# Lightning attention and four summed experts on one core: values of a chunk and scores of the next in one TensorE run

## Chip, core and metric

The kernel runs on one core of one Trainium2 chip. The metric is the device time of one execution in microseconds (us). Three timed executions before the change took 1149.92, 1150.4 and 1151.87 us, so the median is 1150.4 us. One further execution was recorded by the hardware profiler; times of single instructions come from that one.

## What is computed

All numbers are fp32. The first block is a linear attention with decay over 4 batches, 8 heads, 768 positions and 64 columns per head, in blocks of 64 positions that pass a 64x64 state per head on:

```python
for b in range(nb):                      # 12 blocks of 64 positions
    intra = einsum('bhic,bhjc->bhij', qb, kb) * Dmask
    intra = einsum('bhij,bhjd->bhid', intra, vb)
    inter = einsum('bhid,bhde->bhie', qb * lam_pow, kv_state)
    out[:, :, sl] = intra + inter
    kv_state = lam_block * kv_state + einsum('bhsd,bhse->bhde', kb * rev_pow, vb)
```

Its output, turned to 3072 tokens of 512 columns, goes through four experts that are all applied and summed with normalised weights:

```python
p = domain_probs / (domain_probs.sum(-1, keepdims=True) + 1e-09)
for e in range(4):
    h = maximum(x @ w1[e], 0.0)          # 512 -> 1024
    out += p[:, e:e + 1] * (h @ w2[e])   # 1024 -> 512
```

## The kernel before

**Tokens and units.** The 24 chunks of 128 tokens (two blocks of 64 each, all eight heads) form three groups of 8 chunks. A unit is one group with one expert, so there are twelve, numbered 0 to 11 in the order in which they run. Both matrix products of a unit are built with Strassen's scheme in Winograd's form: seven products M1 to M7 of operands that are blocks (A11, A12, A22, B11 and so on) or sums of blocks (S1 to S4 and T1 to T4). The first product (`x @ w1`) carries the scheme two levels deep. The second product (`h @ w2`) has one level in units 0 to 4 and two levels ("nested") from unit 5 on.

**Steps and slots.** TensorE's order is written out by hand in the main loop. While unit `at` does its second product, the next unit does its first. Each unit has seven steps `i`, one for a product of each kind, and each step has eight slots `x`. In units 0 to 4 the even slots 0, 2, 4 and 6 each hold a quarter of the second product (`part`, matmuls of line 1175) and the odd slots hold two of the first product's inner products (`inner`, line 1116; slot 5 holds only one). So a unit has 56 slots, and slot number `(at * 7 + i) * 8 + x` counts through all units. Behind a slot's matmuls the loop issues at most a few waiting pieces of VectorE work, then the attention steps that stand at this slot, then due transfers (`pump`).

**Waiting VectorE work.** `lately` holds the attention's pieces, `background` the operands of later products and sums, `own_sums` operand sums of the first product. In units 0 to 3 one piece of `lately` is issued in each slot if there is one; then one of `background` if nothing was taken, if `fits()` (a planner's account of VectorE time, `filled`, is less than 0.6 slots ahead) or if more than one is queued; then `own_sums` under the like rule. What a product needs and has not been issued is forced at the product (`rest(force=True)`).

**Second product's order.** `SEQ2` is M1, M7, M4, M6, M2, M5, M3. M1, M6, M5 and M3 add up in PSUM banks `q01` and `q11`; M7, M4 add up in `q02` and `q12`, and M2 uses these two banks afresh. `part` (line 1175) evicts every quarter with a VectorE instruction of 128x256 (lines 1189 and 1193). `later_operands` (L899 on) queues S2 at step M4, S1 at step M2 and S4 at step M5, four VectorE instructions of 128x512 each; S4 takes S2 out of use. For unit 4 S4 goes through PSUM banks `q02` and `q12` (`through`).

**Attention of the groups 1 and 2** (chunks 8 to 23) is spread over units 0 to 3, one chunk every 12 slots from slot 24 (`BEGIN`). With s the chunk's slot:

- s - 10: `load_more` issues the loads of q and k on the SP queue (for group 2 transposed copies `qx` and `kx` and a plain k); s - 6: the load of v.
- s: `turn`. For group 1 TensorE transposes q and k into banks `s0` and `s1` (line 691), ScalarE copies both out (lines 699, 700), VectorE makes `qs`, the decayed q, from PSUM, and GpSimd decays k (`decayed`). For group 2 VectorE transposes `qx` and `kx` (line 673) and makes `qs`; k's decay is issued at s - 2. GpSimd carries a chunk's state on (`begin_state`).
- s + 5 (s + 6 in group 2): `scores`, 64 records of 64x64 matmuls into `s0` and `s1` (lines 721 and 728): q against k, and k against v for the state. Its VectorE pieces are masking (two instructions), `middle` (adds to the state) and `end` (state times decay, then an addition: two instructions of 128x256).
- s + 10 (s + 12 in group 2): `values`, 64 records of 64x64 matmuls into `s0` and `s1` (lines 775 and 793). ScalarE copies the output (line 814), VectorE adds what lies apart (`adds`). After every second chunk GpSimd and SP make and store operand sums (`pair_sums`), which `x_fill` reads back later.

A trace record is half of an fp32 matmul instruction, so four matmuls show as x8. All tiles of 128x512 named `small` share one pool of 42 buffers; a state is one such tile with two halves.

Of the kernel before, what the change touches and what calls it, by code (L numbers as in the profile page):

```python
# [21 lines left out]
def kernel(  # L22
# [456 lines left out]
    def comes_across(n):  # L479
        return where(n)[0] >= SECOND  # L480
# [150 lines left out]
    def fits():  # L631
        return filled[0] - now[0] < 0.6

    def rest(n=1, force=False):
        for _ in range(n):
            take(background, force)
# [18 lines left out]

    def begin_state(n):
        if where(n)[0] == 0 and n not in states:
            states[n] = small("kv")[:].rearrange("p (x h d) -> p x h d", x=2, d=D)
        if where(n)[0] and n in states and n not in carried:
            carried.add(n)  # L660
            passed(nc.gpsimd, states[n][:, 1], states[n][:, 0])

    def turn_across(n):

        qT, kT = nat.pop((n, "qx")), nat.pop((n, "kx"))
        qs = small("qs")

        def scaled():
            scale_q(qs, qT)
            turned[n] = qT, kT, qs  # L670

        def across(x):
            nc.vector.transpose(out=x[:], in_=x[:])
            vector(W, False)

        soon(n, *(lambda x=x: across(x) for x in (qT, kT)), scaled)

    def turn(n, tags):
        all_added()
        begin_state(n)  # L680
        if comes_across(n):
            turn_across(n)
            return
        if n < CPG:
            decayed(n)
        qn, kn = nat.pop((n, "q")), nat[n, "k"]
        qp = bank(tags[0], "qp")
        kp = bank(tags[1], "kp")
        for x, y in ((qp, qn), (kp, kn)):
            for ac in range(NHP):  # L690
                nc.tensor.transpose(  # L691
                    out=x[:, ac * C:(ac + 1) * C], in_=y[:, 2 * ac:2 * ac + 2].rearrange("p r d -> p (r d)"),
                    identity=ident[:],
                )
        if n >= CPG:
            decayed(n)
        del nat[n, "k"]
        qT, kT, qs = small("qT"), small("kT"), small("qs")
        nc.scalar.copy(out=qT[:], in_=qp[:])
        nc.scalar.copy(out=kT[:], in_=kp[:])  # L700
        scaled = lambda: scale_q(qs, qp)
        soon(n, scaled)
        turned[n] = qT, kT, qs, scaled

    def scores(n, tags):
        all_added()
        while n not in turned:
            take(lately, True)
        qT, kT = turned[n][0:2]
        while any(f in lately for f in turned[n][3:]):  # L710
            take(lately, True)
        begin_state(n)
        kd, vn = nat.pop((n, "kd")), nat[n, "v"]
        first, last = where(n)[0] == 0, where(n)[0] == NCH - 1

        sp = [bank(tags[r], "sp") for r in range(2)]
        blk = [slice(x * BL, (x + 1) * BL) for x in range(2)]
        for ac in range(NHP):
            for r in range(2):
                for x in range(2):  # L720
                    nc.tensor.matmul(  # L721
                        out=sp[r][half[x], ac * BL:(ac + 1) * BL], lhsT=hc(kT)[half[r], ac, blk[x]],
                        rhs=hc(qT)[half[r], ac, blk[x]], start=(ac == 0), stop=True, skip_group_check=True,
                    )
        for ac in range(NHP):
            for x in range(1 if last else 2):
                for r in range(2):
                    nc.tensor.matmul(  # L728
                        out=sp[x][half[r], 256 + ac * D:256 + (ac + 1) * D], lhsT=kd[half[x], 2 * ac + r],
                        rhs=vn[half[x], 4 * r + ac], start=False, stop=True, skip_group_check=True,  # L730
                    )
        st = small("st")
        added = [sp[x][:, 256:512].rearrange("p (h d) -> p h d", d=D) for x in range(2)]

        def mask(r):
            tt(
                nc.vector, st[:, r * 256:(r + 1) * 256], sp[r][:, 0:256], s_decay[:, r].rearrange("p h c -> p (h c)"),
                ALU.mult,
            )

        def middle():
            s = states[n][:, 1]
            if first:
                nc.scalar.copy(out=s, in_=added[0])
            else:
                tt(nc.vector, s, s, added[0], ALU.add)

        def end():
            s = states[after_of(n)] = small("kv")[:].rearrange("p (x h d) -> p x h d", x=2, d=D)
            passed(nc.vector, s[:, 0], states[n][:, 1])  # L750
            tt(nc.vector, s[:, 0], s[:, 0], added[1], ALU.add)

        work = [lambda: (mask(0), mask(1)), middle] + ([] if last else [end])
        soon(n, *work)
        masked[n] = st, work

    def values(n, tags):
# [15 lines left out]
        def inter(a, r, x, start):  # L773
            for y in range(2):
                nc.tensor.matmul(  # L775
                    out=op[r][half[y], cols(a, r) if x == r else apart(a)], lhsT=state[half[r], x, 2 * a + y],
                    rhs=by_block(qs)[half[r], 2 * a + y, x], start=start, stop=False, skip_group_check=True,
                )

# [56 lines left out]
        ))  # L836

    FILL = {1: 18, 2: 43}
    BEGIN = {1: (24, 12), 2: (24 + 12 * CPG, 12)}
    steps = []  # L840

    def attention(g):

        def put(slot, f):
            steps.append((slot, f))

        for i in range(CPG):
            n, s = g * CPG + i, BEGIN[g][0] + BEGIN[g][1] * i
            put(s - 10, lambda n=n: load_more(n))
            put(s - 6, lambda n=n: load(n, "v"))  # L850
            put(s, lambda n=n: turn(n, ("s0", "s1")))
            if comes_across(n):
                put(s - 2, lambda n=n: (decayed(n), nat.pop((n, "k"))))
            put(s + (6 if comes_across(n) else 5), lambda n=n: scores(n, ("s0", "s1")))
            put(s + (12 if comes_across(n) else 10), lambda n=n: values(n, ("s0", "s1")))
            if n == NG * CPG - 1:
                put(s + 17, turn_gates)
        steps.sort(key=lambda s: s[0])

    def forget():  # L860
        while lately:
            take(lately, True)
        assert not states


    rows = {
# [3 lines left out]
    def operands(key):  # L870
# [6 lines left out]

        background.append(step)

    def later_operands(g, e, m):  # L880

        def step(h, a):
            if m == "M4":
                t = h["S2"] = h.pop("S3")
                tt(nc.vector, t[:], a[:], t[:], ALU.subtract)
# [2 lines left out]
                tt(nc.vector, t[:], h["S2"][:], t[:], ALU.add)  # L888
            else:
                t = h["S4"] = h.pop("A12")  # L890
                tt(nc.vector, t[:], t[:], h.pop("S2")[:], ALU.subtract)

        def through(hs):
            up = [None] * 4
# [4 lines left out]

            def less(x):  # L900
                t = hs[x]["S4"] = hs[x].pop("A12")
                tt(nc.vector, t[:], up[x][:], hs[x].pop("S2")[:], ALU.subtract)
                if x < 2:
                    bring(x + 2)

# [1 line left out]
            bring(1)  # L907
            background.extend(lambda x=x: less(x) for x in range(4))

        if m == "M5" and unit_of[g, e] == NEST - 1:  # L910
            through([hid[g, e, uu, sj] for sj in (1, 0) for uu in range(2)])
        elif m in ("M4", "M2", "M5"):
            for sj in (1, 0):
                for uu in range(2):
                    h = hid[g, e, uu, sj]
                    background.append(lambda h=h, a=h["A22"] if m == "M4" else None: step(h, a))

    outer = {e: {n: {} for n in ("B11", "B12", "B21", "B22", "T1", "T2", "T3", "T4")} for e in range(NEST, len(units))}
    within = {}
# [218 lines left out]


    acc = {}  # L1140
    SEQ2 = ("M1", "M7", "M4", "M6", "M2", "M5", "M3")
    ADD = {"M1": (0, 0), "M2": (0, 0), "M7": (1, 1), "M6": (1, 0), "M4": (1, 0), "M5": (1, 1), "M3": (0, 1)}
    fed2 = {}

# [15 lines left out]
    def second_product(g, e, m, banks):  # L1160
# [36 lines left out]

        def done():
            del fed2[g, e, m]
            if m in ("M4", "M5", "M3"):  # L1200
                for uu in range(2):
                    for sj in range(2):
# [566 lines left out]
        "M2": ((), (), (("M3", 0, 0), ("M3", 0, 1)), (), (("M3", 1, 0), ("M3", 1, 1))),  # L1769
        "M4": ((("M5", 0),), (("M5", 1),), (("M2", 0),), (("M2", 1),)),  # L1770
    }
    for g in range(1, NG):
        attention(g)
    PACE = 1.0, 1.0, 1.0
    FEED = (1, 5), (2, 5)
    first_steps = first_result()
# [2 lines left out]
    for at, (g, e) in enumerate(units):  # L1779
# [9 lines left out]
            chores.extend(prepare_w2_ops(1, True))  # L1789
            spare.append(True)  # L1790
        if at == NEST - 1:
            forget()
            packed.append(True)
        blocks, banks = {}, {}
        for i in range(7):
# [41 lines left out]
            for x, part in enumerate(order):  # L1837
# [15 lines left out]
                    pass  # L1853
                elif (ahead or x % 2 == 0 and x + i) and not (nests and i == 6 and x == 7):
                    if nested or nests:
                        rest()
                        if at == 2 * E and i in (2, 3) and fits():
                            rest()
                    else:
                        took = False  # L1860
                        for of in (lately, background, own_sums):
                            if of and (not took or fits() or of is background and len(of) > 1):
                                take(of)
                                took = True
                if nested or nests:
                    take(aside)
                    if own_sums and (nested or fits()):
# [19 lines left out]
                        x_fill(h, SEQ[at * 7 + i - FILL[h]])  # L1887
                pump(PACE[g])
    pump(force=True)
    assert not (first_steps or ending or background or aside or chores or queue or late or results)  # L1890


# [26 lines left out]
```

## Time and profile before

| what | value |
|---|---|
| three timed executions | 1149.92, 1150.4, 1151.87 us; median 1150.4 |
| the profiled execution's own time | 1154.07 us |
| its span in the trace | 1152.3 us (1.8 us lie around it) |
| mean granted TensorE clock | 0.997 |
| busy TensorE (PE), VectorE (DVE), ScalarE (ACT), GpSimd (POOL) | 1141.1, 768.8, 379.4, 771.2 us |
| units 0 to 4 in the span | 90.60 to 593.1 us |
| matmul records of lines 721, 728, 775 and 793 | 768, 704, 704, 768, about two thirds of them of groups 1 and 2 |

The span runs from the first to the last instruction. "PE" is the row of matmuls, "PEld" that of weight loads, "SPq" the queue of SyncE, which issues nearly all transfers in the order of the program. The ends of matmuls are modelled, so distances on PE are best read from start to start. In a row of the timeline the first number is the start, the second the length, and xN the number of records merged. In the view by windows, each row is a stretch with its length and then busy time and number of records for each engine.

### The profile page before, as it was taken

What the parts mean: (1) busy time and instruction counts of PE and PEld (TensorE: products, weight loads), DVE (VectorE), ACT (ScalarE), POOL (GpSimd) and SP (SyncE); (2) the same over time, 40 slices, a digit from 0 to 9 for tenths busy, and PEclk for the clock granted to TensorE, in tenths of its full rate; (3) what the DMA queues carried; (4) which work ended last, traced back from release to release, by engine and by line L of the source; (5) the groups of instructions that cost most, each with busy time, mean ns of one, the idle gap of its engine ahead of it and who ended that gap; (6) DMA issues with size and microseconds to landing.
All of it is one profiled execution on the core that took longest, in us unless ns stands there. A gap on an engine that the chain in (4) does not pass through costs nothing.

```text
span 1152.3 us, 22188 instructions
## 1 busy us (share of the span) xinstructions
PE 1141.1 (99%) x8015; PEld 992.5 (86%) x8015; DVE 768.8 (67%) x1426; ACT 379.4 (33%) x764; POOL 771.2 (67%) x734
## 2 busy tenths in 40 slices
PE   8999999999999999999999999999999999999998
PEld 6788888888888888888888888888888888888887
DVE  4576775468478747945774666778766566776785
ACT  3412123212311321222344453344345442342332
POOL 2747417646752965773886798795895783883885
PEclk8999999999999999999999999999999999999999
DMA  9795667999999989987877658986678756647552
GB/s 197 181 285 153 180 192 226 302 286 294 285 301 318 274 268 297 295 288 240 247 226 228 221 179 270 326 261 208 200 245 280 217 172 188 206 160 208 176 192 74
DMA packets 309148, 269.22 MB, mean 234 GB/s; under 512 B 141424, under 2 KB 244016, under 8 KB 309040
## 3 DMA queue, kind: packets, MB, share of 16 engines
q1 hardware_dynamic: 291360, 262.66, 73.6%
q10 hardware_dynamic: 17648, 5.15, 2.1%
q8 instruction: 64, 1.05, 0.4%
q14 instruction: 44, 0.36, 0.1%
q0 software_dynamic: 32, 0.00, 0.0%
HBM read 194.83 MB, written 77.10 MB: 236 GB/s over the span
## 4 chain that ended last, share of the span: by engine, by line
PE 95%; POOL 2%; DVE 1%; issue 1%; DMA 0%; ACT 0%; DVEq 0%; POOLq 0%
PE pg L1116 39%; PE pq L1478 23%; PE q L1175 21%; PE pM L1620 3%; PE pc L1620 2%; PE sp L721 1%; PE op L775 1%; PE op L793 1%; PE sp L728 1%; POOL acc L117 1%; PE qp L691 1%; PE pM L1345 1%; DVE m L117 1%; PE kp L691 1%; PE pg L1478 1%
## 5 line engine op out<-in xcount | busy, mean ns | idle before, releaser
L1116 PE MATMUL pg<-xs,ws_in 128*128 128x256 f32 x1960 | 472.3, 381 | 0.9 <-DVE m L117 0.8
L1116 PEld LDWEIGHTS pg<-xs,ws_in 128*128 128x128 f32 x1960 | 369.1, 190 | 54.6 <-DVE m L117 3.5
L117 DVE TENSOR_TENSOR m<-pg,m 128x512 f32<-128x512 f32 x374 | 255.4, 686 | 101.5 <-PE pg L1116 91.2
L1175 PE MATMUL q<-w2t,m 128*128 128x256 f32 x1120 | 265.4, 380 | 0.0
L1175 PEld LDWEIGHTS q<-w2t,m 128*128 128x128 f32 x1120 | 212.1, 190 | 29.1
L117 DVE TENSOR_TENSOR sums<-pq,sums 128x256 f32<-128x256 f32 x272 | 113.0, 420 | 90.3 <-PE pq L1478 78.1
L117 POOL TENSOR_TENSOR m<-m,decay 128x512 f32<-128x512 f32 x91 | 114.7, 1273 | 81.8 <-ACT m L1133 66.8
L1478 PE MATMUL pq<-acc,w2t 128*128 128x256 f32 x688 | 169.2, 379 | 0.0
L1478 PEld LDWEIGHTS pq<-acc,w2t 128*128 128x128 f32 x688 | 130.5, 190 | 18.0
L1133 ACT ACTIVATE m<-m 128x512 f32<-128x512 f32 x99 | 62.4, 630 | 185.2 <-DVE m L117 182.6
L1193 DVE SCALAR_TENSOR_TENSOR acc<-q,gate,acc 128x256 f32<-128x256 f32 x108 | 51.9, 481 | 74.8 <-PE q L1175 74.5
L117 DVE TENSOR_TENSOR m<-m,m 128x512 f32<-128x512 f32 x108 | 95.4, 884 | 6.0 <-ACT m L1099 5.9
L1129 ACT COPY m<-pg 128x512 f32<-128x512 f32 x88 | 51.6, 586 | 121.0 <-PE pg L1116 116.6
L1093 ACT COPY pg<-m 128x512 f32<-128x512 f32 x77 | 45.4, 590 | 124.6 <-DVE m L117 124.5
L117 POOL TENSOR_TENSOR acc<-hT,hT 128x512 f32<-128x512 f32 x56 | 70.4, 1274 | 22.7 <-DVE hT L117 12.5
L117 POOL TENSOR_TENSOR acc<-hT,acc 128x512 f32<-128x512 f32 x56 | 71.3, 1273 | 6.5 <-PE pq L1478 2.7
L1478 PE MATMUL pq<-hT,w2t 128*128 128x256 f32 x288 | 70.0, 379 | 0.0
L117 POOL TENSOR_TENSOR w2o<-w2b 128x512 f32<-128x512 f32 x26 | 35.0, 1365 | 46.8 <-DMA w2b<-in_moe_w_dram 28.4
L1478 PEld LDWEIGHTS pq<-hT,w2t 128*128 128x128 f32 x288 | 54.7, 190 | 7.4
L1478 PE MATMUL pq<-m,w2t 128*128 128x256 f32 x228 | 55.4, 379 | 0.0
L947 ACT COPY hp<-m 128x512 f32<-128x512 f32 x84 | 48.5, 589 | 16.3 <-DVE hT L117 15.2
L1097 ACT COPY m<-pg 128x512 f32<-128x512 f32 x44 | 25.8, 586 | 84.3 <-PE pg L1116 76.9
(152 smaller groups left out, 1435.3 us busy)
## 6 DMA issues: line engine op xcount, KB each, us to landing
w2t<-w_ops SPq DMA_DIRECT2D x129, 256.0 KB, 3.1
ws_in<-w_ops SPq DMA_DIRECT2D x40, 512.0 KB, 4.3
ws_in<-w_ops SPq DMA_DIRECT2D x60, 256.0 KB, 3.8
ws_in<-w_ops SPq DMA_DIRECT2D x40, 384.0 KB, 4.0
w2b<-in_moe_w_dram SPq DMA_DIRECT2D x56, 256.0 KB, 5.1
w_ops<-ops SPq DMA_DIRECT2D x28, 512.0 KB, 4.9
w2t<-w_sums SPq DMA_DIRECT2D x40, 256.0 KB, 4.1
w_sums<-w2o SPq DMA_DIRECT2D x16, 512.0 KB, 5.3
```

What stands on the lines that cost most here:

```text
L117: eng.tensor_tensor(out=o, in0=a, in1=b, op=op)
L691: nc.tensor.transpose(out=x[:, ac * C:(ac + 1) * C], in_=y[:, 2 * ac:2 * ac + 2].rearrange("p r d -> p (r d)"), identity=ident[:],)
L947: nc.scalar.copy(out=there[x][:], in_=blk[at][:])
L1093: nc.scalar.copy(out=banks[tags[1]][:], in_=new["11"][:])
L1097: nc.scalar.copy(out=o[:], in_=p[:])
L1116: nc.tensor.matmul(out=p[:, j * 256:(j + 1) * 256], lhsT=ws[i][:, j * P:(j + 1) * P], rhs=xs[i], start=(fresh and j == 0), stop=True, skip ...
L1129: nc.scalar.copy(out=new[at][:], in_=p[:])
L1133: nc.scalar.activation(out=new[at][:], in_=new[at][:], func=AF.Relu)
L1175: nc.tensor.matmul(out=p[:, s * DH:(s + 1) * DH], lhsT=h[A_OF[m]][:, c * 256 + s * P:c * 256 + (s + 1) * P], rhs=fed2[g, e, m][uu][:, c], ...
L1193: nc.vector.scalar_tensor_tensor(out=o, in0=x, scalar=w, in1=o, op0=ALU.mult, op1=ALU.add)
L1478: nc.tensor.matmul(out=p[:, 0:256], lhsT=fed3[e, m, x // 2][:, x % 2, c * P:(c + 1) * P], rhs=b[B_OF[i]][:, c * 256:(c + 1) * 256], start= ...
L1620: nc.tensor.matmul(out=p[:, s * 256:(s + 1) * 256], lhsT=a[c][:, f:f + P], rhs=b[:, c, j * 256:(j + 1) * 256], start=(s == 0 and c == 0 an ...
```

## The change

The attention of groups 1 and 2 gets a new table of slots, `AT`, one entry for each of the 16 chunks. At a chunk's entry stands one run that holds the values of the chunk before (banks `s0`, `s1`) and then the scores of this chunk (now in banks `q02`, `q12`). The first run holds only scores, and the last values come 5 slots after the last run. The second product's order becomes M1, M7, M4, M2, M6, M5, M3, so that `q02` and `q12` are unused in the steps M6, M5, M3 and the next unit's M1; all entries of `AT` lie there.

Around it:

- q is scaled in place (`scale_q(qT, qT)`), as a fourth VectorE piece behind the scores, so there is no tile `qs` for groups 1 and 2.
- `end` is four `scalar_tensor_tensor` of 128x64 (state times decay plus the addition in one) in place of two `tensor_tensor` of 128x256, in all three groups.
- A state is held as two half tiles that share a buffer with those of other chunks (`state_half`).
- Loads of q and k stand 5 slots ahead of `turn`, `turn` 4 slots (group 2: 6) ahead of the run, the load of v 5 slots ahead of the run, k's decay in group 2 one slot ahead of `turn`.
- S2 and S1 are both queued at step M4 in units 1 to 4 (in unit 0 S1 waits for step M2), S4 at step M6; S2 lives until both M6 and S4 have used it (`spent`).
- `background` is issued beside another piece only if it fits or if more than four are queued (one before); unit 0 issues `own_sums` in the even slots of step 1; in unit 4 `lately` goes first.

```diff
-        qT, kT, qs = small("qT"), small("kT"), small("qs")
+        qT, kT = small("qT"), small("kT")
...
+        if n >= CPG:
+            turned[n] = qT, kT, qT
+            return
...
-            s = states[after_of(n)] = small("kv")[:].rearrange("p (x h d) -> p x h d", x=2, d=D)
-            passed(nc.vector, s[:, 0], states[n][:, 1])
-            tt(nc.vector, s[:, 0], s[:, 0], added[1], ALU.add)
+            s = state_half(0)
+            states[after_of(n)] = {0: s}
+            for ac in range(NHP):
+                vector(D, True)
+                nc.vector.scalar_tensor_tensor(
+                    out=s[:, ac], in0=states[n][1][:, ac], scalar=q_decay[:, ac, BL - 1:BL], in1=added[1][:, ac],
+                    op0=ALU.mult, op1=ALU.add,
+                )
...
         work = [lambda: (mask(0), mask(1)), middle] + ([] if last else [end])
+        if n >= CPG:
+            work.append(lambda: scale_q(qT, qT))
...
-    BEGIN = {1: (24, 12), 2: (24 + 12 * CPG, 12)}
+    AT = (34, 42, 50, 58, 89, 95, 102, 108, 114, 146, 153, 165, 171, 202, 209, 221)
...
-            put(s - 10, lambda n=n: load_more(n))
-            put(s - 6, lambda n=n: load(n, "v"))
-            put(s, lambda n=n: turn(n, ("s0", "s1")))
+            s = AT[n - first]
+            turns_at = s - (6 if comes_across(n) else 4)
+
+            def both(n=n):
+                if n > first:
+                    values(n - 1, ("s0", "s1"))
+                scores(n, ("q02", "q12"))
+
+            steps.append((turns_at - 5, lambda n=n: load_more(n)))
+            steps.append((s - 5, lambda n=n: load(n, "v")))
+            steps.append((turns_at, lambda n=n: turn(n, ("s0", "s1"))))
             if comes_across(n):
-                put(s - 2, lambda n=n: (decayed(n), nat.pop((n, "k"))))
-            put(s + (6 if comes_across(n) else 5), lambda n=n: scores(n, ("s0", "s1")))
-            put(s + (12 if comes_across(n) else 10), lambda n=n: values(n, ("s0", "s1")))
+                steps.append((turns_at - 1, lambda n=n: (decayed(n), nat.pop((n, "k")))))
+            steps.append((s, both))
+        steps.append((AT[last - first] + 5, lambda: values(last, ("s0", "s1"))))
...
-        elif m in ("M4", "M2", "M5"):
...
+        elif m in ("M4", "M2", "M6"):
+            ahead = unit_of[g, e] > 0
+            for by in {"M4": ("M4", "M2")[:1 + ahead], "M2": ("M2",)[ahead:], "M6": ("M6",)}[m]:
...
-    SEQ2 = ("M1", "M7", "M4", "M6", "M2", "M5", "M3")
+    SEQ2 = ("M1", "M7", "M4", "M2", "M6", "M5", "M3")
...
-                            if of and (not took or fits() or of is background and len(of) > 1):
+                            if of and (not took or fits() or of is background and len(of) > 4):
                                 take(of)
                                 took = True
+                        if at == 0 and i == 1 and x % 2 == 0:
+                            take(own_sums)
```

## The prediction

> **What bounds the kernel now.** I read the page's totals first, then the chain of work that ended last, then the view by windows with one window for each step of units 0 to 4, then the timeline of TensorE around one attention run.
>
> ```profile
> PE 1141.1 (99%) x8015; PEld 992.5 (86%) x8015; DVE 768.8 (67%) x1426; ACT 379.4 (33%) x764; POOL 771.2 (67%) x734
> ...
> PE 95%; POOL 2%; DVE 1%; issue 1%; DMA 0%; ACT 0%; DVEq 0%; POOLq 0%
> ```
>
> TensorE is busy for 99% of the span, and 95% of the chain is its own work. The 2% of POOL is a stretch at 726 to 746 us that starts from TensorE's own results (GpSimd is idle for 6.0 us there before them), so no other engine carries a clock of its own: what TensorE saves in units 0 to 4 should arrive at the end. The windows tell what attention costs there:
>
> ```profile
> 515.39:528.34 12.95, 12.95 (x61) 11.40 (x60) 3.32 (x6) 3.52 (x6) 6.50 (x8) 1.00 0.97 326
> 312.49:326.73 14.24, 14.24 (x126) 12.34 (x125) 6.38 (x11) 3.52 (x6) 10.16 (x14) 1.00 0.93 290
> 205.44:220.97 15.53, 15.53 (x189) 13.28 (x188) 5.62 (x13) 4.29 (x10) 11.55 (x16) 1.00 0.99 312
> 370.72:384.96 14.24, 14.24 (x126) 12.34 (x124) 13.57 (x25) 5.64 (x12) 13.61 (x16) 1.00 0.99 283
> 473.20:488.09 14.89, 14.49 (x109) 12.25 (x108) 14.43 (x22) 4.86 (x8) 13.30 (x12) 1.00 0.79 269
> ```
>
> The first number behind the stretch is its length. A step without attention takes 12.95 us (60 records), with one run 14.24, with two 15.53: a run costs 1.29 us, and nothing waits. The last row alone is longer than its content (14.24) by 0.65 us; there VectorE is busy for 14.43 us. At 13.57 of 14.24 us (the row above) nothing was lost. Why a run costs 1.29 us is in the timeline (start, length, then the instruction):
>
> ```profile
> 137.24 1.89 PE L1175 MATMUL q<-w2t,m 128*128 128x256 f32 x8
> 138.96 1.03 PE L1116 MATMUL pg<-xs,ops 128*128 128x256 f32 x4
> 139.92 0.69 PE L721 MATMUL sp<-qT,kT 64*64 64x64 f32 x32
> 140.43 0.65 PE L728 MATMUL sp<-vn,kn 64*64 64x64 f32 x32
> 141.01 1.99 PE L1175 MATMUL q<-w2t,m 128*128 128x256 f32 x8
> 142.84 1.03 PE L1116 MATMUL pg<-xs,ops 128*128 128x256 f32 x4
> ```
>
> From start to start, 8 large records take 1.73 us undisturbed (137.24 to 138.96) and 32 small ones 0.51. Four large ones should end at 139.82, but the run starts at 139.92 (0.10 lost); its second half takes 0.58 until the next large one (0.07 lost); that one's eight take 1.83 (0.10 lost). So 64 small records cost 2 x 0.51 = 1.03 us, and going from 128x128 to 64x64 and back costs 0.26, which is 1.29 less 1.03.
>
> **The change, part by part.**
>
> *Fewer runs.* Before, 16 chunks have two runs each: 32. After, there are 16 entries and a last run of values: 17. The records stay the same. 15 x 0.26 = **3.9 us less** on TensorE. Between values and scores inside a run nothing need be lost: between the halves of present runs the distance is 0.51, as inside them.
>
> *Transposes, ScalarE copies, masks, adds* stay as they are. Scaling q costs VectorE 776 ns from SBUF (the row of `qs<-qx`) in place of 683 from PSUM for the 8 chunks of group 1: 0.7 us in all, spread over VectorE's idle time. It counts only if VectorE is late (below).
>
> *`end`.* The two instructions now cost 502 + 415 = 917 ns. Four of 128x64 have no row. From 128x256 at 416 and 128x128 at 282 ns (`st<-sp` and `xc<-xc,op`) a straight line gives 215; the fused form at 128x256 takes 481, 65 more. So 4 x 215 to 4 x 280 = 0.86 to 1.12 us, between 0.06 less and 0.2 more for each of 20 chunks. I take 1.0. In the opening (chunks 0 to 7) the state is read four chunks later, so this lies beside other work.
>
> *VectorE by step.* This decides whether evictions stay in time. A step has up to 6 evictions of 686 ns and 4 of 481: 6.0 us. The heaviest new steps: in units 1 to 3, step M4 queues eight operands at once, 8 x 0.884 = 7.1, so 13.1 us of 12.95; step M6 of unit 3 holds two runs (15.5 us less 0.26, as one of the two is joined: 15.3) with 6.0, four S4 (3.5), one S3 (0.9), masks, `middle`, `end`, scaling and a transpose (3.7) and adds (0.7): 14.8. By the rows above 95% was free and 101% cost 0.65 us. Three steps at 101% for up to 0.65 each: 0 to 2 us; the deadlines of these operands lie one and two steps later, so an overflow can drain in step M2 (6.0 + 3.5 of 12.95). I take 0.5. In return S4 leaves the step at 473.20 for the one ahead, and its 0.65 should go: -0.6 (bounds -0.8, with 0.1 more in the step at 488.09, and 0).
>
> *Waits that are new.* Chunk 16's run at slot 114 finds the second transpose of its inputs issued in that very slot (`lately` holds four pieces of chunk 15, then two transposes, one a slot from 109): behind the slot's 0.48 eviction and 0.70 of its own it is ready some 1.2 to 1.4 us after the slot's matmuls, and TensorE has 1.1 us of values ahead of it: 0 to 0.3 us, once. The next product in `q02` and `q12` (M7) starts at least five slots after the last scores, for three slots of pieces; M2's last evictions are three to four slots old when scores come. TensorE is in order, so anything late here holds all large matmuls behind it.
>
> *Loads.* Five slots now lie between the issue of q and k and their transposes (8.1 us, with a run between them 10.4), ten before. SP issues in order, and it is often behind:
>
> ```profile
> 155.12 0.93 SPq L174 DMA_DIRECT2D qn<-in_q_dram  x2
> 164.02 0.92 SPq L174 DMA_DIRECT2D kn<-in_k_dram  x2
> ...
> 187.05 0.98 SPq L174 DMA_DIRECT2D qn<-in_q_dram  x2
> 188.13 1.00 SPq L174 DMA_DIRECT2D kn<-in_k_dram  x2
> ```
>
> Set against the time at which TensorE passed the slot of the issue, k of chunks 8 to 15 had left SP at -1.3, -3.5, 7.0, 8.3, 3.2, 8.0, 1.8, 2.0 us (chunk 10: slot 38 ended at 158.0 on TensorE, k's second issue at 164.9). A k load lands 4.4 us (median) after its issue, some 3.9 after the end of the issue; its transposes come 10.8 us (10.4 and 0.4 of q's) after the slot. So a chunk waits for lag - 6.9: the same lags at the same chunks would cost 0.1 + 1.4 + 1.1 = 2.6 us. For v the room is 9.6 us in group 2; its largest lag, 9.4 us at chunk 23, would cost 3.8, and no other any. Bounds 0 and 6.4. Chunk 10's lag is a wait of 7.9 us for a buffer that the scores of chunk 9 free; its load now stands ahead of those scores, so it takes another. Chunk 11's place hardly moves (slot 50 to 49), so it may be late again; 12's and 13's move to where lags were 2 to 4. I take 0.5.
>
> *The rest.* `pair_sums` come at other slots, seven of eight later, but their reader (`x_fill`, from slots 147 and 347 on) has 33 slots and more behind the last of them (114 and 226). S2's longer life and the shared half tiles against 16 tiles `qs` less: no wait on a buffer stands on the chain now, and SP's are in the item above.
>
> **Sum:** -3.9 + 0.5 - 0.6 + 0.5 = **-3.5 us**. The profiled execution took 1154.07 us (span 1152.3 and 1.8 around it), so 1150.6 by its own time; it is 3.7 above the median, and I take the difference over: 1150.4 - 3.5 = **1146.9**, 0.3% less. A measurement of this kernel can tell about 0.2% (2.3 us) from no change.
>
> **Rivals.**
>
> 1. *VectorE falls behind.* For: 13.1 of 12.95 us in step M4, 14.8 of 15.3 in step M6, against a 0.65 us loss at 14.43 of 14.24. Against: the totals stay, and the steps after M4 are light. At 0.65 in each of four dense steps 2.6, none saved at 473.20: 1150.4 - 3.9 + 2.6 = 1149.1, no change to be seen. Chance 0.15.
> 2. *Loads come late* (the side of slower). SP's lag stays what it was, chunks 10, 11 and 13 and the v of a late chunk wait: 6.4 us, 1150.4 - 3.9 + 6.4 = 1152.9. It decides from lags of about 7 us on (5.6 for v), and the change loses once the waits exceed 3.9. For: SP issues back to back in units 1 to 3, with DMA shares of 0.9 to 1.0. Against: only 3 of 8 k loads were so late, one of them for a cause that goes. Chance 0.12.
> 3. *The 0.26 is not of the change of size* but a start of each part of attention (its semaphores), and stays: 1150.4. Against: the transposes, which are 128x128 and wait for data of their own, lose 0.00 us on entry and exit, and one half of a run follows the other without loss. [...] Chance 0.05.
>
> The forecast has 0.68, within 1145.5 and 1148.1. The range of 8 in 10 reaches up through rival 1 and to 3: **1145.5 to 1150.5**. Faster by over 0.2% (below 1148.1) has the forecast's 0.68; slower 0.10, most of rival 2; within 0.2% the other 0.22.
>
> **What the profile of the changed kernel would show.** Steps with one joined run at 12.95 + 2.06 + 0.26 = 15.27 us (16.1 with transposes), and none of 14.24 but the first and last run's. The saving right: units 0 to 4 shorter by 3.5 us. Wrong by rival 1: TensorE idle behind VectorE at lines 1116 or 1175 in steps M4 and M6. By rival 2: TensorE idle at line 691 or 728 behind a DMA of `qn`, `kn` or `vn`. By rival 3: joined runs of 2.6 us. Wrong in a way I do not see: later units longer than before.

## Result and profile after

The kernel after the change takes **1157.77 us** (median of 7, 1155.83 to 1159.57), the kernel before 1150.49 us beside it (1149.64 to 1155.52, 7 runs). The ratio is 1.0053, 95% interval 1.0036 to 1.0071: slower by 0.5%, where 0.3% faster was forecast. The medians lie 7.3 us apart; the ratio goes by the means of the runs and is worth 6.1 us. The profiled execution took 1156.1 us, its span is 1154.3 us.

The page's totals, and the first line of the chain of work that ended last:

```profile
PE 1137.0 (98%) x8015; PEld 992.5 (86%) x8015; DVE 774.8 (67%) x1466; ACT 378.5 (33%) x764; POOL 771.3 (67%) x734
...
PE 70%; POOL 1%; DVE 1%; issue 1%; ACT 0%; POOLq 0%; DVEq 0%
```

TensorE has 4.1 us less to do than before, yet the kernel is longer: what it saves stands beside new idle time. The chain, which was 95% PE, breaks off and sums to 73%. So I measured the seven steps of every unit by the view with one window for each step. Units 0 to 3, unit 4 up to its last step (i = 6), and the rest from that step to the start of the last group of matmuls, in us:

| | unit 0 | unit 1 | unit 2 | unit 3 | unit 4, i = 0 to 5 | sum | rest |
|---|---|---|---|---|---|---|---|
| before | 99.73 | 106.63 | 102.48 | 103.00 | 77.70 | 489.54 | 567.76 |
| after | 101.66 | 113.28 | 100.70 | 99.62 | 78.99 | 494.25 | 567.83 |

The rest does not move, so time saved or lost in units 0 to 4 reaches the end whole. (The opening ahead of unit 0, 90.60 us before and 87.86 after, is not in the table; more on it at the sum below.) Units 2 and 3 are faster, units 0 and 1 slower. The steps that show why (stretch, length; then busy us and records of PE, PEld, DVE, ACT, POOL; granted clock, DMA share, GB/s):

```profile
244.42:269.55 25.13, 19.09 (x325) 16.45 (x323) 12.21 (x26) 4.91 (x14) 8.12 (x10) 0.91 0.72 218
269.55:286.75 17.20, 17.20 (x198) 15.00 (x197) 12.23 (x26) 5.81 (x13) 8.22 (x8) 0.94 0.79 234
373.18:388.34 15.16, 15.16 (x174) 13.26 (x172) 12.97 (x25) 5.26 (x12) 10.81 (x12) 1.00 0.90 263
472.80:487.96 15.16, 15.16 (x174) 13.27 (x173) 13.79 (x24) 5.41 (x13) 11.23 (x11) 1.00 0.78 244
```

A step with one joined run and nothing else takes 15.16 us (the last two rows), so a joined run costs 2.21 over the bare 12.95. Two separate runs cost 2 x 1.29 = 2.58. **Each join saves 0.37 us**, and 15 joins 5.5. With transposes at 0.87 the content of each step is known, and what exceeds it is waiting: 0.85 in unit 0, i = 1 (no attention, 12.95; it took 13.80); 0.94 in the step from 172.55 (one joined run and transposes, 16.03; it took 16.97); 6.89 in the step at 244.42 (two joined runs and transposes, 18.24); 1.17 in the next (16.03); 0.34 in the step from 302.80, 0.86 from 331.25, and 0.12 from 457.52, where a transpose for the gates stands that is in the like sum for before too. Together 11.2. Before, the like sum is 1.0. So -5.5 + 11.2 - 1.0 = **+4.7**, which is 494.25 - 489.54.

One place holds 8.06 of the 11.2. TensorE there (start, length, instruction; in brackets its idle time before and what ended it):

```profile
260.73 0.69 PE L793 MATMUL op<-qT,kv 64*64 64x64 f32 x32
...
261.71 0.65 PE L731 MATMUL sp<-qT,kT 64*64 64x64 f32 x32
268.40 1.23 PE L738 MATMUL sp<-vn,kn 64*64 64x64 f32 x32 [6.04 <-DMA vn<-in_v_dram]
269.55 3.04 PE L1202 MATMUL q<-w2t,m 128*128 128x256 f32 x8
```

The last quarter of the run of slot 95 waits 6.04 us for v of chunk 13. And when it has come, the 32 small records take 1.15 us to the next start and the 8 large 2.88, where 0.58 and 1.73 are usual. SP's queue tells why v was late:

```profile
239.51 0.56 SPq L114 DMA_DIRECT2D across<-in_k_dram  x1
248.69 1.98 SPq L174 DMA_DIRECT2D qn<-in_q_dram  x2
...
262.06 0.38 SPq L114 DMA_DIRECT2D vn<-in_v_dram  x1
```

Between 240.07 and 248.69 SP issues nothing. Its own row in the view of waits names the cause (total, times, longest):

```profile
SPq L174 <- PE op L793: 8.6, 1, 8.6
```

Line 793 is a product of `values`. The load of chunk 13's q, issued at slot 86, needs one of the 42 buffers, and by this row it gets one only when the values of chunk 11 free theirs. TensorE reaches those at 247.97 (slot 89). Chunk 11 was scored at slot 58 (`AT` goes from 58 to 89): its qT, masked scores, v and state halves sat in the pool for 31 slots, since values now come only with the next scores. SP issued nothing else in these 8.6 us, so all loads of weights behind this one stood too. The DMA view of 240 to 275 us in forty slices:

```profile
DMA  9999400000060889969999999999999678965697
GB/s 392 321 354 383 111 0 0 0 0 0 19 137 16 183 190 401 295 185 236 330 365 379 295 313 376 419 411 385 337 305 224 139 176 180 291 207 143 194 295 219
```

For about five us nothing moves; then the arrears are worked off at full load, v leaves at 262.06, 1.3 us after its run has begun, and takes until 268.4.

### The profile page after: what moved, and what is told of

Read it like the earlier page. It is cut to its first block, busy times and chain, and to the rows that moved or that the text cites. A ratio compares the mean times of both kernels' runs of the same rounds, so it can differ in the third digit from the quotient of the medians.

```text
span 1154.3 us, 22193 instructions
## 1 busy us (share of the span) xinstructions
PE 1137.0 (98%) x8015; PEld 992.5 (86%) x8015; DVE 774.8 (67%) x1466; ACT 378.5 (33%) x764; POOL 771.3 (67%) x734
## 4 chain that ended last, share of the span: by engine, by line
PE 70%; POOL 1%; DVE 1%; issue 1%; ACT 0%; POOLq 0%; DVEq 0%
PE pg L1143 32%; PE pq L1509 24%; PE q L1202 12%; DVE m L117 1%; POOL acc L117 1%; PE pM L1376 1%; PE pg L1509 1%; PE op L793 0%; PE sp L731 0%; POOL m L117 0%; PE op L811 0%; PE sp L738 0%; PE yp L1336 0%; PE yp L1409 0%; DVE acc L1220 0%
## 5 line engine op out<-in xcount | busy, mean ns | idle before, releaser
L117 DVE TENSOR_TENSOR m<-m,m 128x512 f32<-128x512 f32 x108 | 91.9, 851 | 6.1 <-ACT m L1126 5.9
L1156 ACT COPY m<-pg 128x512 f32<-128x512 f32 x88 | 51.5, 586 | 127.2 <-PE pg L1143 118.5
L117 POOL TENSOR_TENSOR kn<-kn,decay 128x512 f32<-128x512 f32 x16 | 17.4, 1088 | 74.2 <-PE kp L697 55.1
```

Source lines behind the costliest of these rows:

```text
L117: eng.tensor_tensor(out=o, in0=a, in1=b, op=op)
L1156: nc.scalar.copy(out=new[at][:], in_=p[:])
```

## The experiments

**Theory:** the joins save 5.5 us, and the loss is loads: an idle SP behind a full pool, and leads that are too short. **Rival A:** VectorE can't keep up with the denser steps, with q scaled late and in place. **Rival B:** the run itself is the cost, not what surrounds it. Times are medians with lowest and highest, ratios against the kernel before on the same chip, whose medians there lie between 1150.21 and 1150.72 us. Where experiments ran on different chips, their distance is given by the ratios.

### 1. Values of three chunks on their own

The three widest gaps in `AT` (58 to 89, 114 to 146, 171 to 202) are closed: these values run 5 slots after their scores and not with the next.

```diff
+    ALONE = 11, 16, 20
...
-                if n > first:
+                if n > first and n - 1 not in ALONE:
                     values(n - 1, ("s0", "s1"))
...
+            if n in ALONE:
+                steps.append((s + 5, lambda n=n: values(n, ("s0", "s1"))))
```

> The changed kernel, but the values of chunks 11, 16 and 20, which wait 31, 32 and 31 slots for the next run, get a run of their own 5 slots after their scores (three more runs, 0.8 us). Theory A (buffers: SP stood 8.6 us on the load of chunk 13's q because all 42 buffers were taken until the values of chunk 11 gave some back, and chunk 13's v behind it came 6 us late): that wait and TensorE's idle 6 us at the run of slot 95 go, with the slow records behind it: 8.0 less and 0.8 more, some 7 us under the changed kernel, near 1150.5. Theory B (the lead of five slots is too short by itself): the load of chunk 13 stays as it was placed, at least 4 us of the wait stay, 1154 or more.

Measured: 1152.81 us (1150.18 to 1155.54), ratio 1.0021 (1.0011 to 1.0031): 5.0 us below the change's 1157.77, with three joins fewer. SP's wait of 8.6 us is gone, v of chunk 13 leaves at 254.49. It still comes too late:

```profile
263.42 0.69 PE L738 MATMUL sp<-vn,kn 64*64 64x64 f32 x32 [1.25 <-DMA vn<-in_v_dram]
```

After this idle time the large records take their usual 1.83 us, at a granted clock of 1.00. The ratios are 0.32% apart, 3.7 us; units 0 to 4 of the trace take 489.27 us, 5.0 less than with the change. That is short of the 7 that theory A expected, since this wait for v stays. What follows: the full pool is the larger part of the loss, and the rest is not in it.

### 2. v ahead of q and k

```diff
-            steps.append((turns_at - 5, lambda n=n: load_more(n)))
-            steps.append((s - 5, lambda n=n: load(n, "v")))
+            steps.append((turns_at - 5, lambda n=n: (load(n, "v"), load_more(n))))
```

> The changed kernel, but v of a chunk is issued in the same slot as q and k and ahead of them. Theory A: SP still stands until the values of chunk 11, but now behind v(13); q and k of chunk 13 land 1 to 2 us after their transposes want them; TensorE's wait of 6 us for vn goes, in its place 1 to 2 us for qn: 5 to 6 us under the changed kernel, near 1152. Theory B: v has four slots more of lead, the wait for it goes, q and k land as before: 1150 to 1151, and SP shows no wait of several us ahead of q(13).

Measured: 1153.05 us (1151.12 to 1155.6), ratio 1.0023 (1.0014 to 1.0032). Now v's load is the one that stands 8.2 us behind line 793, and v is there when it is needed. Yet unit 1 is no better than 112.44 us, since TensorE stands still in the same run:

```profile
265.35 0.91 PE L738 MATMUL sp<-vn,kn 64*64 64x64 f32 x21 [3.92 <-issue]
266.19 3.78 PE L1201 MATMUL q<-w2t,m 128*128 128x256 f32 x8
```

"issue" means that nothing the profile shows held it (more on this at the end), and the eight large records then take 3.57 us. Moving v alone does not empty the pool; in the median 4.7 us went all the same. In the profiled execution units 0 to 4 gain only 0.7 us (493.60), so the medians and this trace do not agree, and the run is inconclusive on the size.

### 3. The joined runs split again

Scores come one slot behind the values, in the new banks; 15 runs more, all else as changed.

```diff
             def both(n=n):
-                if n > first:
-                    values(n - 1, ("s0", "s1"))
                 scores(n, ("q02", "q12"))
...
-            steps.append((s, both))
+            if n > first:
+                steps.append((s, lambda n=n: values(n - 1, ("s0", "s1"))))
+            steps.append((s + (n > first), both))
```

> The changed kernel, but scores stand one slot behind the values of the chunk before, in a run of their own, with large matmuls between: 15 runs more. If going to 64x64 and back costs 0.26 us a run, TensorE's own work grows by 3.9 us; the scores come one slot (1.6 us) later, so the wait for vn of chunk 13 shrinks by up to 1.6: together 2.3 to 3.9 us over the changed kernel, 1160 to 1161.7. If that 0.26 is a start cost of each part, nothing grows: 1156 to 1158.

Measured: 1162.46 us (1160.26 to 1163.69), ratio 1.0101 (1.0086 to 1.0116): 4.7 above the change, over the 2.3 to 3.9 expected; by the ratios 0.48%, 5.5 us, near 15 x 0.37 = 5.5 (its v wait is 4.36 in place of 6.04, and 1.9 us of waits for a scaled q are new). Rival B falls: joining gains, and more than forecast.

### 4. The kernel before with the short leads

Only the old kernel's loads are moved: q and k 5 slots ahead of `turn` (10 before), v 5 ahead of the scores (11 or 12), k's decay 1 ahead of `turn`.

```diff
-            put(s - 10, lambda n=n: load_more(n))
-            put(s - 6, lambda n=n: load(n, "v"))
+            put(s - 5, lambda n=n: load_more(n))
+            put(s + (1 if comes_across(n) else 0), lambda n=n: load(n, "v"))
...
-                put(s - 2, lambda n=n: (decayed(n), nat.pop((n, "k"))))
+                put(s - 1, lambda n=n: (decayed(n), nat.pop((n, "k"))))
```

> The kernel before, with the short leads of the changed one: q and k loaded 5 slots ahead of the transposes in place of 10, v 5 slots ahead of the scores in place of 11 (12), k's decay one slot ahead in place of two. Buffers are taken later and given back as before, so there is less pressure on the 42. Theory A: SP is not held for buffers, waits for loads stay under 1 us in all: 1150 to 1151.5. Theory B: TensorE waits for qn, kn or vn at several chunks, 3 to 6 us: 1153.5 to 1156.5.

Measured: 1155.02 us (1153.77 to 1156.39), ratio 1.0040 (1.0027 to 1.0052). **4.4 us for the leads alone**, with no join and no new bank. In the trace one wait stands out:

```profile
185.75 0.46 PE L728 MATMUL sp<-vn,kn 64*64 64x64 f32 x16 [2.77 <-DMA vn<-in_v_dram]
```

This v left SP at 181.57, behind stores that waited for their data and a load that waited 2.0 us for such a store to land, and arrived 4.2 us later.

### 5, 6 and 7. Longer leads, on top of the first experiment

All three kernels keep `ALONE`. In 5 the loads stand eight slots ahead:

```diff
-            steps.append((turns_at - 5, lambda n=n: load_more(n)))
-            steps.append((s - 5, lambda n=n: load(n, "v")))
+            steps.append((turns_at - 8, lambda n=n: load_more(n)))
+            steps.append((s - 8, lambda n=n: load(n, "v")))
```

> The kernel with values of chunks 11, 16 and 20 alone, and with the loads of q and k 8 slots ahead of turn in place of 5 and of v 8 ahead of the run in place of 5. Both causes taken away together (buffers come free, and loads have 4.9 us more): no wait of TensorE for qn, kn or vn over 0.5 us. 12 joins are left, 0.37 us each by the steps of 15.16 us in the changed kernel's trace: 4.4 us; waits on VectorE of some 2 us stay. 1147 to 1148.5. If something else than buffers and lead makes the changed kernel slow, it stays over 1150.

In 6 eleven:

```diff
+            steps.append((turns_at - 11, lambda n=n: load_more(n)))
+            steps.append((s - 11, lambda n=n: load(n, "v")))
```

> As the one before, with 11 slots of lead for both, longer than in the kernel before. If lead is still what is short at 8 slots, this is faster than that one by up to 1 us. If buffers are, loads that ask for them earlier find none, SP stands for several us again, and this one is slower than that by 1 to 5 us.

In 7 the change's five, with v ahead of q and k:

```diff
+            steps.append((turns_at - 5, lambda n=n: (load(n, "v"), load_more(n))))
```

> Values of 11, 16 and 20 alone, and v issued in the slot of q and k ahead of them, the leads of q and k left at five slots. The wait of 1.4 us for chunk 13's v goes; q and k of chunk 11 stay late (1.2 us, as in the changed kernel), others may wait a little more, since v is ahead of them on SP. 1150 to 1152, if q and k are short by lead; 1148 or less if v alone was.

Measured: eight slots **1146.70 us** (1144.31 to 1147.12), ratio 0.9963 (0.9951 to 0.9975), faster than both kernels; eleven slots 1150.31 (1146.67 to 1155.52), 1.0001 (0.9989 to 1.0013); v with q and k 1150.85 (1148.42 to 1153.4), 1.0005 (0.9996 to 1.0014). Eight slots came out just below the 1147 to 1148.5 expected. With eight, the last part of the run of slot 95 has nothing to wait for:

```profile
260.01 0.65 PE L738 MATMUL sp<-vn,kn 64*64 64x64 f32 x32
260.59 1.99 PE L1205 MATMUL q<-w2t,m 128*128 128x256 f32 x8
```

and no wait for a load is left in units 0 to 3. Units 0 to 4 take 486.37 us, 3.2 less than before; 12 joins by 0.37 are 4.4, and some 2.2 of waits remain against 1.0. Eleven slots give it back. SP stands for a buffer again, though for 4.5 us once (behind line 731) and without a late load in this trace. There a run waits for k's decay on GpSimd, behind sums that GpSimd does ahead of it, and unit 2 takes 102.49 in place of 100.77:

```profile
391.60 0.68 PE L738 MATMUL sp<-vn,kn 64*64 64x64 f32 x16 [1.08 <-POOL kn L117]
```

Why eleven cost all 3.6 us in the median I can't say; its profiled execution, whose units 0 to 4 take 487.5, shows 1.1 of them. Seven falls where q and k were to be short by lead. In its trace the step of chunk 11's transposes is again 1.35 us over its content; the row there names ScalarE, but its copy and the landing of q end within 0.1 us of each other, so the two are not told apart. The longer lead without the first experiment was not tried.

### 8 to 12. Rival A: is the rest of the change free?

In 8 the whole change is kept, but attention goes back to the old slots, banks and leads, with nothing joined. 9, 10 and 11 take single edits out of it, 12 does 9's to the best version.

```diff
-            s = AT[n - first]
...
+            s, x = 24 + 12 * (n - CPG), comes_across(n)
+            steps.append((s - 10, lambda n=n: load_more(n)))
+            steps.append((s - 6, lambda n=n: load(n, "v")))
+            steps.append((s, lambda n=n: turn(n, ("s0", "s1"))))
...
+            steps.append((s + 5 + x, lambda n=n: scores(n, ("s0", "s1"))))
+            steps.append((s + 10 + 2 * x, lambda n=n: values(n, ("s0", "s1"))))
```

> The changed kernel with the attention back on the slots, leads and banks of the kernel before, so that no run is joined: what is left is the new order of the second product, its operands, the scaling in place, the four small instructions of end, the half tiles and the rule for waiting pieces. If all of these are free, as the prediction had it, 1150 to 1151. If the order and the bunched operands cost VectorE time that TensorE waits for, 1152 or more.

Measured: 1155.59 us (1153.26 to 1157.06), ratio 1.0040 (1.0028 to 1.0052). I had held the rest to be free; on the old slots it costs about 5 us. Windows of this kernel: step M4 of unit 2, where eight operands are queued, and step M2 of unit 1, behind such an M4:

```profile
324.40:340.73 16.33, 14.51 (x125) 12.26 (x124) 14.29 (x25) 1.85 (x6) 9.82 (x7) 1.00 1.01 302
232.88:248.62 15.74, 15.18 (x134) 13.17 (x133) 13.46 (x25) 4.18 (x10) 9.49 (x7) 1.00 0.96 288
```

Their contents are 14.24 and 15.11. The timeline inside the first:

```profile
336.50 1.35 DVE L117 TENSOR_TENSOR m<-m,m 128x512 f32<-128x512 f32 x1
...
338.90 1.99 PE L1135 MATMUL pg<-xs,ws_in 128*128 128x256 f32 x8 [1.82 <-DVE m L117]
```

An operand sum, 0.88 us in my working, takes 1.35 here, and TensorE stands 1.82 us until the eviction behind it has run. Two edits are suspects: eight operands at once, and the scaling of q as the last piece behind the scores. In experiment 9 S1 waits for M2 again:

```diff
-            ahead = unit_of[g, e] > 0
+            ahead = False
```

> The kernel with the whole change but attention on the old slots (1155.6, 4.9 above the kernel before), and one edit undone: the S1 operands are queued at M2 again and not together with S2 at M4, so no step has eight operands at once. If the bunched operands are what VectorE cannot take in (step M4 of units 1 to 3: 16.33 for a content of 14.24 at 324 us, 15.74 for 15.53 at 221 us), 2 to 3 us of the 4.9 go: 1152.6 to 1153.6, and the step at 324 us takes 14.3 to 14.6. If it is the scaling of q in place and late, which the values wait for, nothing moves: 1155 to 1156.

In 10 q is scaled straight after its transposes into a tile of its own, as before:

```diff
...
-            turned[n] = qT, kT, qT
-            return
...
-            work.append(lambda: scale_q(qT, qT))
```

> The same kernel on the old slots, with q scaled into a tile of its own straight after its transposes, as before, and the bunched operands kept. If scaling in place behind the masks is the cost (steps with values longer by 0.1 to 0.4 us each, behind a wait for VectorE's qT), 1 to 2.5 us go: 1153 to 1154.6, and no weight load of the values waits for VectorE. If the bunched operands are, the step at 324 us keeps its 16.3 and the time stays within 1 us of 1155.6.

In 11 both, and the older rule for a second piece:

```diff
-                            if of and (not took or fits() or of is background and len(of) > 4):
+                            if of and (not took or fits() or of is background and len(of) > 1):
```

> The same kernel on the old slots with both undone, and with the older rule by which a second operation is taken from the queue of operands (more than one left, not more than four). What stays of the change is the order of the second product, the state in halves with `end` in four pieces, and no transposed q scaled early. If the two edits are the whole cost, 1150 to 1151.5, the time of the kernel before; what stays above that (up to 4.9) belongs to the order of the products and to `end`.

(The 15.74 us that the expectation of 9 gives to a step M4 are those of this step M2, from 232.88, with its content of 15.11; M4 of unit 1, from 217.76, took 15.12.)

Measured: 9 gives 1153.02 us (1151.87 to 1158.8), ratio 1.0022 (1.0010 to 1.0035); 10 gives 1151.17 (1149.83 to 1154.04), 1.0006 (0.9994 to 1.0017); 11 gives **1150.40** (1149.39 to 1152.93), 1.0002 (0.9991 to 1.0013). The same two steps in 9 and then in 10:

```profile
332.06:346.29 14.23, 14.23 (x125) 12.34 (x124) 11.26 (x22) 1.85 (x6) 7.14 (x6) 1.00 1.03 326
239.38:255.38 16.00, 15.19 (x134) 13.17 (x133) 13.48 (x25) 4.19 (x10) 8.04 (x7) 1.00 0.93 276
```

```profile
324.28:338.52 14.24, 14.24 (x126) 12.34 (x125) 11.97 (x24) 1.85 (x6) 7.04 (x6) 1.00 1.00 331
233.64:248.75 15.11, 15.11 (x133) 13.17 (x132) 11.68 (x25) 4.19 (x10) 7.34 (x6) 1.00 0.89 260
```

Either edit undone frees the first step; only 10 frees the second. There, in 9, the waits say what is late (total, times, longest):

```profile
PEld op L793 <- DVE qT L117: 3.0, 3, 1.2
```

The values wait for the scaled q, five slots behind the scores, with three pieces and the adds ahead of the scaling. So on the old slots the scaling costs: by the ratios 1.0040 - 1.0006 = 0.34%, 3.9 us. For the operands it is 0.18%, 2.1 us, which is less certain, since the intervals of 8 and 9 overlap; for both with the rule 0.38%, 4.4 us. The two costs are not separate sums: the first step is freed by either. With both undone, the time of the kernel before is back, so the order M2 before M6, the half states and the new `end` cost nothing that can be measured.

Does that hold on the new slots? Experiment 12 is the best version with S1 at M2.

> The best version so far (1146.7: values of three chunks alone, loads eight slots ahead) with S1 queued at M2 again. If the bunched operands cost the same there as on the old slots, 1144 to 1145.5; if the joined runs already lie where VectorE has room, no change: 1146 to 1147.5; if S1 at M2 now meets the masks of joined runs, up to 1 us slower.

Measured: 1148.22 us (1146.29 to 1149.77), ratio 0.9979 (0.9968 to 0.9991), beside 0.9963 (0.9951 to 0.9975) for the best version: no gain, and whether it is slower the intervals, which overlap, do not say. In this version the eight operands cost nothing that can be seen, and values lie six slots or more behind their scores (the last five); in the kernel after no matmul waited for a scaled q. Rival A is a cost of these edits on the old slots, and of 1.7 us at most in the change itself.

## Why the prediction was wrong

It forecast 1146.9 within 1145.5 and 1150.5 and gave slower a chance of 0.10. The term that failed is **Loads**: it was set at 0.5 us and measured 9.0. Two sentences made it so, one in it and one in *The rest*, on which it leans.

*"I take 0.5"* (bounds 0 to 6.4) carried the old lags over to the new slots. Shorter leads cost 4.4 us on the old kernel alone (experiment 4). I had listed the lags and saw 6.4 as the upper end, but argued from how few of them were long. With 16 chunks on one TensorE, which ran nothing else in the 6.04 us that it waited for v, one long lag is enough: 1.4 us at chunk 11 came as worked out (0.94 of it, behind q and then k), and a worse one at chunk 13, which I took for safe:

```profile
186.52 0.63 PE L697 MATMUL qp<-ident,qn 128*128 128x128 f32 x4 [0.36 <-DMA qn<-in_q_dram]
```

*"no wait on a buffer stands on the chain now"* reasoned from what the old kernel waited for. What the change does to the pool was to be read from `AT`: values move to the next chunk's slot, so where two entries lie 31 slots apart a chunk's tiles stay 31 slots. SP then stood 8.6 us, and TensorE lost 6.04 by waiting and 1.7 at the granted clock of 0.50 that followed. This is rival 2, loads that come late, by a road that I had excluded; its 1152.9 was 4.9 us too low. With both causes removed, experiment 5 lands on 1146.70, beside the forecast 1146.9, but by another sum: 12 joins at 0.37 less 1.2 of added waits, and not 15 at 0.26. That the two agree is chance.

Term by term, forecast against the trace:

- *Fewer runs*, -3.9: **-5.5**. The saving is there, and rival 3 is out (split again in experiment 3, the runs cost 4.7 us); what goes into the 0.37 us that each run less saves, no row shows. The size was off because I took 0.51 us for each part of a run, which is the first part's. In a joined run only that one takes it:

```profile
161.77 0.69 PE L793 MATMUL op<-qT,kv 64*64 64x64 f32 x32
162.29 0.65 PE L811 MATMUL op<-st,vn 64*64 64x64 f32 x32
162.75 0.65 PE L731 MATMUL sp<-qT,kT 64*64 64x64 f32 x32
163.22 0.65 PE L738 MATMUL sp<-vn,kn 64*64 64x64 f32 x32
163.80 1.13 PE L1143 MATMUL pg<-xs,ops 128*128 128x256 f32 x4
```

  From start to start 0.52, 0.46, 0.47 and 0.58. At 0.465 for a part in the middle, 2.21 - 4 x 0.465 = 0.35 is the price of a run, and 1.29 - 2 x 0.465 = 0.36 before.
- *The stall at 473.20*, -0.6: it went, and with it 0.24 at 384.96; with the transpose for the gates, which stands in another step now, -1.0. The row at 472.80 above has DVE 13.79 of 15.16 us and no wait.
- *VectorE by step*, +0.5: +0.86 in step M4 of unit 2 as feared, none in the M4 steps of units 1 and 3 nor in M6 of unit 3. Rival 1 was right as to kind and small. Another 0.85, together 1.7, lies in step 1 of unit 0, which I had passed over. The new rule issues `own_sums` on VectorE there, but two things end last within 0.02 us, an eviction of VectorE's and an operand from GpSimd. The weight load names GpSimd, as it does there in every kernel with the change:

```profile
112.78 0.73 PEld L1143 LDWEIGHTS pg<-xs,ops 128*128 128x128 f32 x4 [0.98 <-POOL ops L117]
```

  Why GpSimd is later there than before stays open.
- *`end`*: four instructions of 266 to 283 ns, 1.1 us against 0.92, at no cost to the end (experiment 11), as forecast.
- *Chunk 16*, 0 to 0.3: 0.34.
- *Loads*, +0.5: 0.94 + 6.89 + 1.17 = +9.0.

Sum by the trace: -5.5 - 1.0 + 1.7 + 0.34 + 9.0 + 0.12 (at 457.52) = +4.7. The medians are 7.3 apart. The 2.6 between (1.4 by the ratio) stay open: the two profiled executions are one of each, 3.7 us above its median before and 1.7 below it after, and their openings differ (unit 0 begins at 90.60 us before and at 87.86 after, where the change does little), so they can't be set against medians that closely. I also took the 3.7 us before for a constant; most of it, 90.60 against 85 to 88 in most other traces, is that opening.

## What to carry to other kernels

Before work is moved later, write down for each buffer when it is taken and when it comes free in the new order, and look for the widest gap: here a full pool stopped the queue that loads for 8.6 us, and with it every transfer behind. A transfer's lead is not slack because the median load arrives early; here the longest lag of the queue set it, and both too short and too long a lead cost us time (4.4 us in experiment 4, 3.6 from eight to eleven slots). When a gain is lost elsewhere, a version with the schedule kept and only the leads changed (4.4 us), and one with the schedule undone and the rest kept (4.9 us), tell where.

## What the runs showed of the hardware

**The clock after an idle time.** Windows around the 6.04 us in the kernel after (the third number from the end is the granted clock):

```profile
266.00:268.40 2.40, 0.00 (x1) 0.03 (x1) 0.00 (x0) 0.00 (x0) 0.00 (x0) 0.50 0.77 180
270.00:271.00 1.00, 1.00 (x4) 0.73 (x4) 0.00 (x0) 0.00 (x0) 0.00 (x0) 0.50 0.96 337
271.50:272.00 0.50, 0.50 (x4) 0.45 (x3) 0.00 (x0) 0.00 (x0) 0.00 (x0) 0.79 0.43 64
```

The granted clock falls from 1.00 to 0.50 some 2.5 us after the last matmul (0.88 in the window of 264.5 to 265.0, so at about 264.9), and comes back at about 271.7, after 3.3 us of work: 6.8 us at 0.50. So this idle time is paid a second time, with 0.57 + 1.15 = 1.7 us. After the idle times of 1.25 us (experiment 1) and 2.77 us (experiment 4) the granted clock stayed at 1.00. The distance of 2.5 us is not fixed: the idle time of 2.77 us is longer and left the clock as it was. In experiment 3, after 4.36 us, the 32 small records behind the wait take 0.82 us to the next start (0.58 usual) and the 8 large ones 3.27 (1.73 usual). If the 0.24 us over come from work at half speed, that began 0.82 - 2 x 0.24 = 0.34 us after the wait had ended, 4.7 us after the last matmul: my estimate from these rows. What sets these lengths, no run shows.

**A halt without a semaphore.** In experiment 2 TensorE stands 3.92 us within a run of small matmuls, and the view names only "issue". Between 258 and 270 us two packets of queue q8 moved, which the page calls an instruction queue; the page of the kernel after counts 64 of them, 16 KB each, and does not say which engine q8 feeds. Whether they have to do with the halt is not shown: in the kernel after three moved between 240 and 275 us, and the one wait of TensorE there is that for v. The halt is read from one trace; no run tested it.

**VectorE beside GpSimd.** In experiment 8 the sum of two operands of 128x512 took 1.35 to 1.39 us (0.88 in the mean in the kernel before) while GpSimd worked on tiles of the same size. That the one slows the other was not tested.
